# Earlier loads for one block, and a last output tile in two column groups: attention with sinks and a window, then a feed-forward layer

## The chip, the cores and the metric

The kernel runs on one NeuronCore of a Trainium2 chip, in one launch. The metric is the device time in microseconds (us); lower is better. A profiled execution also gives a span, from its first to its last instruction, which is about 2 us shorter than its time.

The engines have their own instruction streams and wait for each other through semaphores: TensorE (PE in the profile; its weight loads are PEld), VectorE (DVE), ScalarE (ACT), GpSimd (POOL) and SyncE (SP). SP computes nothing here; it issues most of the transfers (DMAs), in program order.

## The reference

Attention over 4 batches, 8 heads, 768 tokens and 64 values per head; each token sees the first 4 tokens (the sinks) and the last 128. Its result, 3072 tokens of 512 values, goes through a two-layer network with 2048 hidden values and the activation h * sigmoid(1.702 h).

```
scores = q @ k.T / 8                       # per batch and head, 768 x 768
keep   = (key < 4) | (0 <= query - key < 128)
a      = softmax(where(keep, scores, -1e9))
x      = (a @ v) as [3072 tokens, 512]
h      = x @ w_in                          # 512 -> 2048
out    = (h * sigmoid(1.702 * h)) @ w_out  # 2048 -> 512
```

All inputs and the output are float32; the kernel computes in float16 with float32 sums.

## The kernel before

The 3072 tokens are cut into 12 blocks of 256, numbered k = 0 to 11; three make a batch. A block goes through these steps, and three blocks are in work at a time (attention of one, first layer of the one before it, second layer of the one before that):

- **Loads.** `load(k)` brings q, k and v from HBM (float32). In blocks 0 to 3 q and k come in two halves of heads each, 256 KB (L389); from block 4 on each is one transfer of 512 KB (L396). v is one transfer of 512 KB in all blocks (L404). There are three slots of float32 buffers, so block 3 writes where block 0 was. SP issues nearly all of them.
- **Casts to float16** (L278), from block 2 on all on POOL, in the order q and k of a block, then v.
- **Turning q and k**, so that the head's values lie on partitions: in blocks 0 to 3 by TensorE transposes (L507) with copies out of PSUM by ACT or DVE (L278, tile `blkT`); from block 4 on by a DMA transpose (L529).
- **Scores** (L589) and scores against the sinks (L547) on TensorE, exp on ACT (L609, L555), the mask on DVE (L616), the product with v (L649), division by the sums on DVE (L667, L669), and turning the result (L688 and L695 in the first blocks, then a DMA transpose, L676).
- **First layer**, `mm1(k)`: matmuls of 256 columns (L716), tanh on ACT (L728), the rest of the activation on DVE (L730).
- **Second layer**, `mm2(k)`: for each of the two halves j of 128 tokens, 16 matmuls of 512 columns into one PSUM bank (L744), a scaling by 0.5 into the float32 tile `osb` (L762 on ACT, L764 on DVE), and two stores of 64 tokens each (L776). Only the very last tile is scaled by ACT and DVE together, each taking 256 of the 512 columns of the same bank; its second store is issued by ACT, all others by SP.

The weights come as eight transfers of 512 KB by POOL's software queue (L349): w0 to w3 are `w_in`, w4 to w7 are `w_out`. Until enough is loaded, TensorE runs matmuls of zeros (L822).

The order of the instructions on each engine is not written down by hand. Every step is entered as an operation with an engine, a length, what it depends on and a priority; the class `Plan` simulates the engines, the PSUM banks and the transfers, takes at each moment the operation with the best priority that could start, and puts the instructions down in that order. The engines then execute them strictly in it. So a change of a dependency or a length can change the order of everything after it.

The transfers have an order of their own (`loads`, sorted by priority: blocks 0 and 1, w0 to w5, block 2, w6 and w7, block 3, block 4 and so on) and gates: for each n from 10 to 31 a load (not a weight) waits until an earlier transfer has landed, the one found by walking back until at least 3.8 us of planned transfer time lie between. For block 3 this gives: q waits for the values of block 2; k and v wait for w6. For block 4, q, k and v wait for the first q piece, the first and the second k piece of block 3, and block 5's q waits for block 3's v. Independent of that, a DMA also waits for the one eight places before it in its kind of queue, whose semaphore it takes over.

Of the kernel before, what the change touches and what calls it, by code (L numbers as in the profile page):

```python
# [14 lines left out]
P = 128  # L15
# [179 lines left out]
def kernel(  # L195
# [69 lines left out]
    def f32(o, i=0):  # L265
        return bank[o.banks[i]]
# [70 lines left out]

    CAST_QK, CAST_V = OPT.get("QK", CAST_QK), OPT.get("V", CAST_V)
    o_w = {}
    loads, gates, o_first = [], [], []  # L340

    def weights(j, at):
        if j < 4:
# [31 lines left out]
    def load(k):  # L375
        b, r = divmod(k, R)
        sl = k % RS
        t0 = r * TB
        prio = load_at(f"a{k}")
        war = reuse("s32", sl) + ([o_m[k - 2, 0][-1]] if k > KT else [])  # L380
        dst, dv = qk32[sl], v32[sl]
        lq = {}
        for e, src in enumerate((q, k_ap)):
            eng, dma = ("ACT", nc.scalar) if k == 0 and e else ("SP", nc.sync)
            lq[e] = []
            if k < KT:
                for h in range(2):
                    def f(e=e, h=h, src=src, dma=dma):
                        return dma.dma_start(  # L389
                            dst[:, e].rearrange("p h i d -> p (h i d)")[:, 512 * h : 512 * h + 512],  # L390
                            src[b, h::2, t0 : t0 + TB].rearrange("p (g i) d -> g p (i d)", i=8),
                        )
                    lq[e].append(op(eng, 450, (700 if k < 2 else 850, 8), f, war, prio=prio + (h / 2 + e / 8 if k == 0 else e / 2 + h / 8), kind="load"))
            else:
                def f(e=e, src=src, dma=dma):
                    return dma.dma_start(dst[:, e], src[b, :, t0 : t0 + TB].rearrange("h (p i) d -> p h i d", i=2))  # L396
                lq[e].append(op(eng, 450, (1850, 64), f, war, prio=prio + e / 2, kind="load"))
            loads.extend(lq[e])
            for o in lq[e]:
                o.begin = 1.0 if k > 1 else 0.0  # L400
            if k == 1:
                o_first.extend(lq[e])
        def lv(dma, h):
            return lambda: dma.dma_start(dv[:, h], v[b, h, t0 : t0 + TB].rearrange("h (p i) d -> p h i d", i=2))  # L404

        o_lv = [op("SP", 450, (1850, 64), lv(nc.sync, slice(0, 8)), war,
                   prio=load_at("a1") + 1.5 + k / 8 if k < 2 else prio + 0.7, kind="load")]
        o_lv[0].begin = 1.0 if k > 1 else 0.0
        loads.append(o_lv[0])

        c16 = qk16[k % RQ]
        war = reuse("qk16", k % RQ)
        if k >= KT:
            C = slots(c16)
            for e in range(2):
                for j in range(2):
                    for i in range(2):
                        def f(eng, e=e, j=j, i=i):
                            copy(eng, C[64 * i : 64 * i + 64, e, :, j].rearrange("s p (h d) -> s p h d", h=2),
                                 dst[64 * j : 64 * j + 64, e, :, i].rearrange("s (p h) d -> s p h d", h=2))  # L420
                        o = plan.any(cast(512, CAST_QK[k]), f, lq[e] + war, prio=nominal(k - 1, -7), kind="cqk")
                        o_cqk[k, 2 * e + j, i] = o
        else:
            C = eights(c16)
            for h in range(2):
                for e in range(2):
                    def f(eng, e=e, h=h):
                        copy(eng, C[:, e, :, :, h].rearrange("s i a d -> s a i d"),
                             dst[:, e].rearrange("s h i d -> s (h i d)").rearrange("s (h a i d) -> s h a i d", h=2, a=4, i=2)[:, h])
                    o_cqk[k, e, h] = plan.any(cast(512, CAST_QK[k]), f, [lq[e][h]] + war,  # L430
                                              prio=nominal(k - 1, -7 + 2 * h) if k else NEVER + h, kind="cqk")
        for o in {id(x): x for (kk, _, _), x in o_cqk.items() if kk == k}.values():
            uses("s32", sl, o)
        w16 = v16[k % RV]
        war = reuse("v16", k % RV)


        w = H // len(o_lv)
        for n, o_l in enumerate(o_lv):
            got = []  # L440
            for j in range(2):
                for i in range(2):
                    def f(eng, j=j, i=i, h=slice(w * n, w * n + w)):
                        copy(eng, w16[64 * i : 64 * i + 64, j, h, 0:D], dv[64 * j : 64 * j + 64, h, i])
                    o = plan.any(cast(D * w, CAST_V[k]), f, [o_l] + war + [o_ones],
                                 prio=(nominal(k - 1, -4) if k else NEVER + 5 + n), kind="cv")
                    got.append(o)
                    uses("s32", sl, o)
            for p in range(w * n // 2, w * n // 2 + w // 2):
                o_cv[k, p] = got  # L450
        if r == 0:
            def f():
                for t in range(2):
                    for i in range(2):
                        nc.gpsimd.tensor_copy(
                            out=vs16[64 * t + 32 * i : 64 * t + 32 * i + 2, b, :, i],
                            in_=w16[64 * t : 64 * t + 2, 0, i::2],
                        )
            o_vs[b] = op("POOL", 1400, 1500, f, [*o_cv[k, 0], *o_cv[k, NP - 1], o_vs0], prio=nominal(k - 1, 0), kind="vs")
            uses("v16", k % RV, o_vs[b])  # L460
# [239 lines left out]
    n_o = [0]  # L700
# [33 lines left out]
    def mm2(k):  # L734
        b, r = divmod(k, R)
        g = gT[k % RG]
        for j in range(2):
            last_tile = k == NK - 1 and j == 1
            holder = []
            prev = None  # L740
            for s in range(NS):
                def f(s=s, j=j, holder=holder):
                    for Fi in (2 * s, 2 * s + 1):
                        nc.tensor.matmul(  # L744
                            f32(holder[0]), g[:, Fi, bass.ts(j, P)], w_out16[:, Fi],
                            start=(Fi == 0), stop=(Fi == NF - 1),
                        )
                deps = [o_g[k, s], o_w[4 + s // 2]] + ([prev] if prev else [])
                o = op("PE", 2 * pe_ns(512), pe_ns(512) + 512 / 2.4 + 166, f, deps,
                       prio=nominal(k + 1, 4 * j + s / 2) + 3, acq=None if s else ("o", 1), kind="mm2")  # L750
                uses("gT", k % RG, o)
                holder.append(o)
                prev = o
            oi = n_o[0] % RO
            n_o[0] += 1
            O = osb[oi]
            row = k * TB + j * P
            war = reuse("osb", oi)

            def f(e, O=O, holder=holder, c=slice(0, d_model)):  # L760
                if e == "ACT":
                    nc.scalar.mul(O[:, c], f32(holder[0])[:, c], 0.5)  # L762
                else:
                    nc.vector.tensor_scalar_mul(O[:, c], f32(holder[0])[:, c], 0.5)  # L764

            prio = nominal(k + 1, 4 * j + 4) + 4
            if not last_tile:
                o_c = [op("ACT", 477, 600, lambda f=f: f("ACT"), [holder[-1]] + war, prio=prio,
                          rel=[(holder[0], 0)], kind="oc")]
            else:  # L770
                o_c = [op(e, 270, 400, lambda f=f, e=e, c=c: f(e, c=c), [holder[-1]] + war, prio=prio, kind="oc")
                       for e, c in (("ACT", slice(0, 256)), ("DVE", slice(256, 512)))]
            for i in range(2):
                eng = "ACT" if last_tile and i else "SP"
                def f(O=O, i=i, row=row, dma=nc.scalar if eng == "ACT" else nc.sync):
                    dma.dma_start(  # L776
                        out[row : row + P, :].rearrange("(p i) f -> i p f", i=2)[i], O[64 * i : 64 * i + 64]
                    )
                o_d = op(eng, 590, (420, 4), f, o_c, prio=prio, kind="out")
                uses("osb", oi, o_d)  # L780
# [24 lines left out]
    for n, o in enumerate(loads):  # L805
        if o is o_w[0]:
            g = o_first[-1]
        elif o.kind == "load" and 10 <= n < 4 + 5 * KT + 8:
            m, ahead = n - 1, 0.0
            while ahead < 3800:  # L810
                ahead += next(iter(loads[m].engs.values()))[1][0]
                m -= 1
            g = loads[m]
        else:
            continue
        o.deps.append(g)
# [57 lines left out]
```

## Time and profile before

| What | Value |
|---|---|
| Median of 4 runs | 225.96 us (225.09 to 226.8) |
| Profiled execution | 226.24 us, span 224.2 us |
| TensorE busy | 217.6 us of the span (97%) |
| L716, L744 (the two layers' matmuls) | 100.3 us and 99.8 us busy |
| DMA moved | 36.36 MB, mean 162 GB/s |
| Last of TensorE, last landing of a store | about 219.45 us, 222.99 us |
| Block 2: v issued by SP, cast by POOL from | 29.37 us, 41.20 us |
| Block 3: q and k issued by SP from, keys cast by POOL until | 41.20 us, 48.97 us |

Busy time of TensorE counts a matmul until its result is written; since matmuls overlap, the sum of its rows is longer than the array's work, and a short hole can be hidden by the drain of the matmul before it. Rows of a timeline are: start, length, engine, line, operation, output and inputs, how many are merged, and in brackets the idle time of the engine before it with what ended it. Rows of waits are: total us, times, longest. Rows of stages give, for each engine, the busy us and in brackets the instructions, and at the end TensorE's clock, the transfers' load and GB/s.

### The profile page before, as it was taken

Reading aid. Unit: us, or ns where it says so; the run is one execution under the profiler, and the core shown is the slowest. Engines: PE = TensorE matmul, PEld = TensorE weight load, DVE = VectorE, ACT = ScalarE, POOL = GpSimd, SP = SyncE. Lnnn points to the kernel's source line nnn. Section 1 sums busy time; section 2 is a strip of 40 time slices with the busy share of each in tenths; the row PEclk is TensorE's granted clock in tenths of the full one; section 3 lists DMA queues with packets and bytes.
Section 4 is the critical chain, followed back from the end, with each engine's and each line's share of the span. In section 5 each row is a group of like instructions: output and inputs, shape, how many; then the busy total and the mean of one; then the engine's idle time right before and its main releaser. Section 6 shows DMA issues by size and latency. Waiting matters only on the chain.

```text
span 224.2 us, 5446 instructions
## 1 busy us (share of the span) xinstructions
PE 217.6 (97%) x2170; PEld 152.9 (68%) x2170; DVE 124.8 (56%) x272; ACT 132.4 (59%) x263; POOL 90.9 (41%) x158
## 2 busy tenths in 40 slices
PE   8999999999999999999999999999999999999991
PEld 8968877566757766766677667657667676666640
DVE  1685865577726755566555664665466565534400
ACT  3398456876648776565576477456567576444310
POOL 8299013538996495814806818408400000000000
PEclk9999999999999999999999999999999999999999
DMA  5999999499996999599399598498641411330232
GB/s 205 338 166 201 195 259 246 128 275 303 291 169 119 274 158 261 154 178 281 86 213 233 74 233 211 89 217 214 124 89 25 84 29 31 76 67 0 50 76 65
DMA packets 65704, 36.36 MB, mean 162 GB/s; under 512 B 27760, under 2 KB 60544, under 8 KB 65680
## 3 DMA queue, kind: packets, MB, share of 16 engines
q1 hardware_dynamic: 61040, 31.07, 58.2%
q0 software_dynamic: 4272, 4.29, 11.7%
q10 hardware_dynamic: 368, 0.66, 0.9%
q8 instruction: 17, 0.28, 0.5%
q14 instruction: 7, 0.06, 0.1%
HBM read 27.36 MB, written 6.29 MB: 150 GB/s over the span
## 4 chain that ended last, share of the span: by engine, by line
PE 93%; ACT 2%; DVE 2%; issue 0%; ACTq 0%
PE bank L716 38%; PE bank L744 36%; PE bank L649 6%; PE bank L589 5%; PE bank L822 4%; PE bank L547 2%; ACT at L609 1%; PE bank L507 1%; PE bank L688 1%; PE bank L582 1%; DVE at L616 1%; DVE xn L669 0%; ACT blkT L278 0%; DVE gT L730 0%; ACT th L728 0%
## 5 line engine op out<-in xcount | busy, mean ns | idle before, releaser
L716 PE MATMUL bank<-xT,w_in 128*128 128x256 f16 x768 | 100.3, 273 | 0.0
L744 PE MATMUL bank<-w_out,gT 128*128 128x512 f16 x384 | 99.8, 379 | 0.0
L730 DVE SCALAR_TENSOR_TENSOR gT<-th,bank 128x512 f16<-128x512 f16 x96 | 65.6, 684 | 46.6 <-ACT th L728 46.0
L716 PEld LDWEIGHTS <-w_in 128*128 128x128 f16 x768 | 72.6, 98 | 22.2 <-issue 2.5
L728 ACT ACTIVATE th<-bank 128x512 f16<-128x512 f32 x96 | 57.8, 602 | 45.1 <-PE bank L716 43.0
L278 POOL CAST qk<-qk 64x512 f16<-64x512 f32 (+1 forms) x73 | 44.5, 610 | 54.9 <-DMA qk<-in_q_dram 47.5
L609 ACT ACTIVATE at<-bank 128x512 f16<-128x512 f32 (+1 forms) x96 | 50.4, 572 | 14.6 <-PE bank L589 14.4
L744 PEld LDWEIGHTS <-gT 128*128 128x128 f16 x384 | 35.5, 98 | 23.1 <-issue 0.3
L616 DVE TENSOR_TENSOR at<-at,bank 128x1024 f16<-128x1024 f16 (+1 forms) x40 | 25.6, 639 | 22.3 <-ACT at L609 22.3
L278 POOL CAST v<-v 64x512 f16<-64x512 f32 x45 | 27.6, 614 | 7.7 <-DMA v<-in_v_dram 5.5
L649 PE MATMUL bank<-v,at 128*128 128x65 f16 x352 | 21.2, 193 | 0.2 <-DVE v L278 0.2
L762 ACT ACTIVATE osb<-bank 128x512 f32<-128x512 f32 (+1 forms) x24 | 14.2, 591 | 12.0 <-PE bank L744 12.0
L649 PEld LDWEIGHTS <-at 128*128 128x128 f16 x352 | 17.5, 98 | 3.7 <-DVE at L616 0.3
L555 ACT ACTIVATE ats<-bank 128x256 f16<-128x256 f32 x32 | 12.6, 394 | 7.6 <-PE bank L547 7.5
L669 DVE TENSOR_TENSOR xb<-bank,rcp 128x256 f16<-128x256 f32 x36 | 15.1, 421 | 0.6
L649 PE MATMUL bank<-vs,ats 128*128 128x65 f16 x128 | 14.8, 193 | 0.0
L667 DVE RECIPROCAL rcp<-bank 128x4 f32<-128x4 f32 x48 | 8.6, 179 | 9.6 <-PE bank L649 8.5
L589 PE MATMUL bank<-blkT 64*128 64x256 f16 x192 | 13.4, 244 | 0.0
L589 PEld LDWEIGHTS <-blkT 64*128 64x128 f16 x256 | 8.0, 94 | 7.7 <-issue 6.7
L649 PEld LDWEIGHTS <-ats 128*128 128x128 f16 x128 | 11.9, 97 | 1.9 <-issue 0.2
L822 PE MATMUL bank<-zero 128*128 128x128 f16 x99 | 8.4, 259 | 1.0 <-DVE zero L291 1.0
L547 PE MATMUL bank<-blkT,ks 128*128 128x256 f16 x32 | 8.7, 272 | 0.1
(41 smaller groups left out, 86.8 us busy)
## 6 DMA issues: line engine op xcount, KB each, us to landing
v<-in_v_dram SPq DMA_DIRECT2D x12, 512.0 KB, 6.8
out_dram<-osb SPq DMA_DIRECT2D x47, 128.0 KB, 2.7
qk<-in_q_dram SPq DMA_DIRECT2D x8, 512.0 KB, 5.2
qk<-in_k_dram SPq DMA_DIRECT2D x8, 512.0 KB, 5.8
qk<-in_q_dram SPq DMA_DIRECT2D x8, 256.0 KB, 4.7
w_in<-in_moe_w_in_dram POOLq DMA_DIRECT2D x4, 512.0 KB, 7.1
w_out<-in_moe_w_out_dram POOLq DMA_DIRECT2D x4, 512.0 KB, 14.8
qk<-in_k_dram SPq DMA_DIRECT2D x6, 256.0 KB, 5.0
```

What stands on the lines that cost most here:

```text
L278: {"POOL": nc.gpsimd.tensor_copy, "DVE": nc.vector.tensor_copy, "ACT": nc.scalar.copy}[e](out=out, in_=in_)
L589: nc.tensor.matmul(f32(o_s, 2 * n + i)[:, c : c + w], src[d, j], Q[d].rearrange("d j s -> d (j s)")[:, q0 : q0 + w], start=k >= KM, stop=T ...
L609: nc.scalar.activation(out=A[:, i, 0:W], in_=f32(o_s, 2 * n + i)[:, 0:W], func=AF.Exp, scale=scale)
L616: nc.vector.tensor_tensor(out=A[:, :, 0:W], in0=A[:, :, 0:W], in1=mask[:, c0 : c0 + W].unsqueeze(1).to_broadcast((P, 2, W)), op=ALU.mult,)
L649: nc.tensor.matmul(avp()[:, j, i], a_, v_, start=(n == 0), stop=(n == len(mms) - 1))
L669: o_n = op("DVE", 300, 425, lambda: nc.vector.tensor_tensor(out=X, in0=avp()[:, :, :, 0:D], in1=rc.to_broadcast((P, 2, 2, D)), op=ALU.mult ...
L716: nc.tensor.matmul(f32(holder[0])[:, bass.ts(e, TB)], w_in16[:, c, bass.ts(Fi, P)], X[:, c] if k < KX else X2[:, :, c], start=(c == 0), st ...
L728: o_t = op("ACT", 477, 600, lambda first=first: nc.scalar.activation(out=th[first.places[0]], in_=f32(first), func=AF.Tanh, scale=0.851), ...
L730: o_g[k, s] = op("DVE", 565, 690, lambda first=first, s=s: nc.vector.scalar_tensor_tensor(out=g[:, 2 * s : 2 * s + 2].rearrange("p a t -> ...
L744: nc.tensor.matmul(f32(holder[0]), g[:, Fi, bass.ts(j, P)], w_out16[:, Fi], start=(Fi == 0), stop=(Fi == NF - 1),)
L762: nc.scalar.mul(O[:, c], f32(holder[0])[:, c], 0.5)
L822: nc.tensor.matmul(warm_bank[:, 0:P], zero, zero, start=True, stop=True)
```

## The change

Two things are changed. First, the gates: only the loads with n from 10 to 22 (those of block 2 among them) keep the rule of 3.8 us. The q and k pieces of block 3 wait for block 2's last key piece alone; v of block 3, the loads of block 4 and q of block 5 have no gate left. Second, the last of the 24 output tiles: its 512 columns are computed as a group of 384 and then one of 128, each 16 matmuls, in two PSUM banks. ACT scales the first and SP stores it (two stores of 64 x 384); DVE scales the second, and SP and ACT store it (64 x 128 each). All other tiles are computed, scaled and stored as before. Weight loads on TensorE grow by 16, matmuls by 16, stores by 2.

```
-        elif o.kind == "load" and 10 <= n < 4 + 5 * KT + 8:
+        elif o.kind == "load" and 10 <= n < 15 + 8:
             m, ahead = n - 1, 0.0
             while ahead < 3800:
                 ahead += next(iter(loads[m].engs.values()))[1][0]
                 m -= 1
             g = loads[m]
+        elif o in o_third:
+            g = o_second[-1]
...
     def mm2(k):
-        for j in range(2):
-            last_tile = k == NK - 1 and j == 1
+        for j, c0, c1 in ((0, 0, 512), (1, 0, 512)) if k < NK - 1 else ((0, 0, 512), (1, 0, 384), (1, 384, 512)):
+            w = c1 - c0
...
                         nc.tensor.matmul(
-                            f32(holder[0]), g[:, Fi, bass.ts(j, P)], w_out16[:, Fi],
+                            f32(holder[0])[:, 0:w], g[:, Fi, bass.ts(j, P)], w_out16[:, Fi, c0:c1],
                             start=(Fi == 0), stop=(Fi == NF - 1),
                         )
...
-                    nc.scalar.mul(O[:, c], f32(holder[0])[:, c], 0.5)
+                    nc.scalar.mul(O[:, c0:c1], f32(holder[0])[:, 0:w], 0.5)
                 else:
-                    nc.vector.tensor_scalar_mul(O[:, c], f32(holder[0])[:, c], 0.5)
+                    nc.vector.tensor_scalar_mul(O[:, c0:c1], f32(holder[0])[:, 0:w], 0.5)
...
-            if not last_tile:
-                o_c = [op("ACT", 477, 600, lambda f=f: f("ACT"), [holder[-1]] + war, prio=prio,
-                          rel=[(holder[0], 0)], kind="oc")]
-            else:
-                o_c = [op(e, 270, 400, lambda f=f, e=e, c=c: f(e, c=c), [holder[-1]] + war, prio=prio, kind="oc")
-                       for e, c in (("ACT", slice(0, 256)), ("DVE", slice(256, 512)))]
+            e = "DVE" if c0 else "ACT"
+            o_c = [op(e, w / 1.2 + 50, w / 1.2 + 170, lambda f=f, e=e: f(e), [holder[-1]] + war, prio=prio,
+                      rel=[(holder[0], 0)], kind="oc")]
             for i in range(2):
-                eng = "ACT" if last_tile and i else "SP"
+                eng = "ACT" if c0 and i else "SP"
```

As the planner sees the loads of block 3 and 4 at other times, it puts the instructions from about 44 us of its plan in another order: on TensorE the transposes of block 3 (L507) stand some places earlier between the score, value and second-layer matmuls of block 2's attention; on ACT a copy into `blkT` stands ahead of the last exp steps of block 2; on DVE copies, masks and reciprocals change places; on SP the first output stores stand behind all of block 4's loads. POOL's order is unchanged.

More of the change, by code (lines that the diff above doesn't have):

```diff
@@ L339 @@
     o_w = {}
-    loads, gates, o_first = [], [], []
+    loads, gates, o_first, o_second, o_third = [], [], [], [], []
     def weights(j, at):
@@ L400, in load @@
                 o.begin = 1.0 if k > 1 else 0.0
-            if k == 1:
-                o_first.extend(lq[e])
+            if k in (1, 2, 3):
+                (o_first, o_second, o_third)[k - 1].extend(lq[e])
         def lv(dma, h):
@@ L736, in mm2 @@
         g = gT[k % RG]
-        for j in range(2):
-            last_tile = k == NK - 1 and j == 1
+        for j, c0, c1 in ((0, 0, 512), (1, 0, 512)) if k < NK - 1 else ((0, 0, 512), (1, 0, 384), (1, 384, 512)):
+            w = c1 - c0
+            last = w < d_model
             holder = []
@@ L741, in mm2, with f @@
             for s in range(NS):
-                def f(s=s, j=j, holder=holder):
+                def f(s=s, j=j, holder=holder, c0=c0, c1=c1, w=w):
                     for Fi in (2 * s, 2 * s + 1):
                         nc.tensor.matmul(
-                            f32(holder[0]), g[:, Fi, bass.ts(j, P)], w_out16[:, Fi],
+                            f32(holder[0])[:, 0:w], g[:, Fi, bass.ts(j, P)], w_out16[:, Fi, c0:c1],
                             start=(Fi == 0), stop=(Fi == NF - 1),
@@ L748, in mm2 @@
                 deps = [o_g[k, s], o_w[4 + s // 2]] + ([prev] if prev else [])
-                o = op("PE", 2 * pe_ns(512), pe_ns(512) + 512 / 2.4 + 166, f, deps,
-                       prio=nominal(k + 1, 4 * j + s / 2) + 3, acq=None if s else ("o", 1), kind="mm2")
+                o = op("PE", 2 * pe_ns(w), pe_ns(w) + w / 2.4 + 166, f, deps,
+                       prio=nominal(k + 1, 4 * j + s / 2) + 3 + c0 / 100 * L, acq=None if s else ("o", 1), kind="mm2")
                 uses("gT", k % RG, o)
@@ L753, in mm2, with f @@
                 prev = o
-            oi = n_o[0] % RO
-            n_o[0] += 1
+            if not c0:
+                oi = n_o[0] % RO
+                n_o[0] += 1
+                war = reuse("osb", oi)
             O = osb[oi]
             row = k * TB + j * P
-            war = reuse("osb", oi)
-            def f(e, O=O, holder=holder, c=slice(0, d_model)):
+            def f(e, O=O, holder=holder, c0=c0, c1=c1, w=w):
                 if e == "ACT":
-                    nc.scalar.mul(O[:, c], f32(holder[0])[:, c], 0.5)
+                    nc.scalar.mul(O[:, c0:c1], f32(holder[0])[:, 0:w], 0.5)
                 else:
-                    nc.vector.tensor_scalar_mul(O[:, c], f32(holder[0])[:, c], 0.5)
+                    nc.vector.tensor_scalar_mul(O[:, c0:c1], f32(holder[0])[:, 0:w], 0.5)
             prio = nominal(k + 1, 4 * j + 4) + 4
-            if not last_tile:
-                o_c = [op("ACT", 477, 600, lambda f=f: f("ACT"), [holder[-1]] + war, prio=prio,
-                          rel=[(holder[0], 0)], kind="oc")]
-            else:
-                o_c = [op(e, 270, 400, lambda f=f, e=e, c=c: f(e, c=c), [holder[-1]] + war, prio=prio, kind="oc")
-                       for e, c in (("ACT", slice(0, 256)), ("DVE", slice(256, 512)))]
+            e = "DVE" if c0 else "ACT"
+            o_c = [op(e, w / 1.2 + 50, w / 1.2 + 170, lambda f=f, e=e: f(e), [holder[-1]] + war, prio=prio,
+                      rel=[(holder[0], 0)], kind="oc")]
             for i in range(2):
-                eng = "ACT" if last_tile and i else "SP"
-                def f(O=O, i=i, row=row, dma=nc.scalar if eng == "ACT" else nc.sync):
+                eng = "ACT" if c0 and i else "SP"
+                def f(O=O, i=i, row=row, c0=c0, c1=c1, dma=nc.scalar if eng == "ACT" else nc.sync):
                     dma.dma_start(
-                        out[row : row + P, :].rearrange("(p i) f -> i p f", i=2)[i], O[64 * i : 64 * i + 64]
+                        out[row : row + P, c0:c1].rearrange("(p i) f -> i p f", i=2)[i], O[64 * i : 64 * i + 64, c0:c1]
                     )
```

## The prediction

> **What bounds the kernel now.** I read the page's engine table first, then TensorE's waits, then three stretches of the timeline: the loads between 28 and 50 us, TensorE around 49 us, and the end.
>
> ```profile
> span 224.2 us, 5446 instructions
> PE 217.6 (97%) x2170; PEld 152.9 (68%) x2170; DVE 124.8 (56%) x272; ACT 132.4 (59%) x263; POOL 90.9 (41%) x158
> ```
>
> TensorE is busy for all but 6.6 us, and 4.7 of those are the end: its last matmul ends at about 219.45 of 224.2. So no change of loads can give much; it can only close the few holes in TensorE's row. In the waits of matmuls and of weight loads between 40 and 50 us one place stands out, the transposes of block 3 (L507):
>
> ```profile
> PE bank L507 <- DVE xn L669: 0.4, 1, 0.4
> PEld L507 <- POOL qk L278: 0.9, 1, 0.9
> ```
>
> The timelines of TensorE and of POOL say what it is:
>
> ```profile
> 47.63 1.02 PE L744 MATMUL bank<-w_out,gT 128*128 128x512 f16 x4
> 49.03 0.62 PE L507 MATMUL bank<-perm,qk 128*128 128x128 f16 x8 [0.38 <-DVE xn L669]
> ```
> ```profile
> 36.52 0.61 POOL L278 CAST qk<-qk 128x512 f16<-128x512 f32 x1 [0.71 <-DMA qk<-in_k_dram]
> 41.20 2.61 POOL L278 CAST v<-v 64x512 f16<-64x512 f32 x4 [4.07 <-DMA v<-in_v_dram]
> 44.31 1.18 POOL L278 CAST qk<-qk 128x512 f16<-128x512 f32 x2 [0.49 <-PE bank L649]
> 46.84 0.61 POOL L278 CAST qk<-qk 128x512 f16<-128x512 f32 x1 [1.35 <-DMA qk<-in_k_dram]
> 48.36 0.61 POOL L278 CAST qk<-qk 128x512 f16<-128x512 f32 x1 [0.91 <-DMA qk<-in_k_dram]
> ```
>
> The last cast of block 3's keys ends at 48.97 and the transposes start at 49.03. Four 512-column matmuls from 47.63 fill the array for 4 x 0.216 = 0.86 us, to 48.49. The hole is 0.54 us (the timeline prints 0.38, since it counts a matmul's drain as busy). The keys are late because of SP's gates, in its own timeline:
>
> ```profile
> 29.37 0.59 SPq L404 DMA_DIRECT2D v<-in_v_dram  x1
> 41.20 1.18 SPq L389 DMA_DIRECT2D qk<-in_q_dram  x2
> 42.48 1.20 SPq L389 DMA_DIRECT2D qk<-in_k_dram  x2
> ```
>
> SP stands from 29.96 to 41.20 for block 2's values (11.8 us from issue to landing). By stages the transfers nearly stop there:
>
> ```profile
> 38.00:39.00 1.00, 1.00 (x15) 0.94 (x14) 1.00 (x2) 0.58 (x1) 0.00 (x0) 1.00 1.06 278
> 39.00:41.20 2.20, 2.20 (x19) 1.41 (x19) 1.03 (x3) 1.53 (x3) 0.00 (x0) 1.00 0.19 48
> 41.20:42.50 1.30, 1.25 (x17) 0.83 (x17) 0.59 (x1) 0.90 (x2) 1.22 (x2) 1.00 0.00 0
> ```
>
> The last number is GB/s: 278, 48, 0. At the end:
>
> ```profile
> 219.47 0.38 ACT L762 ACTIVATE osb<-bank 128x256 f32<-128x256 f32 x1 [2.85 <-PE bank L744]
> 219.89 0.42 DVE L764 TENSOR_SCALAR osb<-bank 128x256 f32<-128x256 f32 x1 [6.87 <-ACT osb L762]
> 220.35 0.56 ACTq L776 DMA_DIRECT2D out_dram<-osb  x1
> ```
>
> The two halves of the last tile are scaled one after the other, DVE waiting for ACT, and both stores (SP's at 220.34, ACT's at 220.35) go out after both.
>
> **What the Trainium skill says.** (1) "PSUM — Partial Sum Buffer", section "PSUM bank collisions raise a hardware error": two engines may not touch one bank together, reads included, so ACT and DVE are ordered against each other. The trace agrees: DVE starts 0.04 us after ACT ends. (2) "TensorE: Matmul & The Clock Gate", section "Wait — 56ns, not 53.3ns?": a warm matmul costs N/2.4 + 2.5 ns. It agrees: 36 matmuls of 512 in 7.78 us are 216 ns each, 8 of 128 columns in 0.45 us are 56. (3) "DMA: Bandwidth & Descriptors", section "Queues, rings and completion order": an engine takes one queue's descriptors in order, and turns between queues. It agrees: block 2's four q and k pieces were all issued by 29.3 and were cast at 32.3, 33.6, 35.2, 36.5, in turn, while the software queue's w_out ran beside them. (4) Same page, "Anatomy of one DMA — SWDGE (gpsimd) path": a DMA's fixed part is mostly the receipt of its last write (told of the software path; no run here splits it). In the trace 128 KB stores take 2.2 to 2.6 us to land, though two issued in a row land only 0.65 apart.
>
> **Part 1, the loads.** Removed: block 3's q and k no longer wait for block 2's values or for w_out's third quarter, and block 3's values, block 4's loads and block 5's q have no gate of this kind. Added: block 3's q and k wait for block 2's last keys, landed by 36.5 (their cast starts at 36.52). SP then issues four pieces at 0.6 us each, 36.5 to 39.0, instead of 41.2 to 43.7. They stand behind block 2's values in SP's queue, so they run when those are done, about 41. A 256 KB piece takes 0.65 to 1.4 us (spacing of the landings of block 3's q, and of block 2's casts): q lands by about 42.5, k by about 44 (before: 48.3). Behind SP's four are v, then block 4's q, k, v, then the first output stores, now after block 4's v. That v waits for block 2's values (its semaphore lane, landed 41.2), so the stores are issuable by 42 to 47; ACT writes the first at 44.05 to 44.7 and needs that slot again three tiles later, so I cost their shift at nothing.
>
> POOL keeps its order: v of block 2 from 41.20 to 43.81, then block 3's four casts at about 0.63 each, done at 46.3 instead of 48.97. POOL is then the limit, not the DMA.
>
> In the changed instruction order TensorE has L507 for q just after the key-sink matmul at 46.14, and for k after that, 46.28 + 0.45 (L507) + 0.11 (L688) + 0.86 (four L744) + 0.37 (L649) = 48.07. The casts are done 1.8 us before: the hole of 0.54 closes. What is late next is DVE's last mask of block 2, for the L649 that follows: it needs ACT's exp, which now stands behind a blkT copy (0.48) and ends at about 48.1; mask 0.59, so 48.75, while TensorE comes at 48.95. Slack 0.2, so between 0 and 0.2 of the 0.54 may come back. Past 50 us I find no hole but the turnaround of each score group, so nothing more is to be won. Part 1: -0.5 us, bounds -0.6 and (rival A) +3.
>
> **Part 2, the last tile.** TensorE: 16 x 162.5 + 16 x 56 = 3.50 us for 16 x 216 = 3.45, so +0.03 to +0.05; the 16 more weight loads are inside the 56 ns (L507's row has one each). On the old clock: the 384 columns are ready at 218.57, ACT scales them from 218.60 in 0.49 (between 0.38 for 256 and 0.60 for 512), SP issues at 219.13 and 219.64 (0.46 and 0.59 each with 0.05 between, as at 216.65). TensorE ends at 219.48, DVE needs no ACT now and takes about 0.30 (its rows of 4 and of 256 elements take 0.18 and 0.42, L667 and L669), ACT issues its 32 KB at 219.82, SP its own only at 220.28, after its two larger ones. So SP's last issue is hardly earlier than today (220.34); the gain is size. Before: the last landing was 220.35 + 2.64 = 222.99. After: the two 96 KB land at about 221.3 and 221.95 (0.65 apart), SP's 32 KB 0.2 later, 222.15; ACT's 219.82 + 2.2 = 222.0. Gain 0.84; if a small store takes the full 2.4 it lands at 222.7, gain 0.3; if nothing queues, 1.0. I take **-0.75**.
>
> **Sum.** -0.5 - 0.75 + 0.04 = -1.2 us. The profiled execution took 226.24 (span 224.2 and 2.0 around it), so 225.0; it lay 0.28 above the median of the four runs, 225.96, which gives **224.7**.
>
> **Rivals.** A measurement of this kernel can tell about 0.5%, 1.13 us, from no change.
> A, slower: block 3's q and k take engine time from block 2's values. Those have no slack: their last cast ends at 43.81 and the first L649 that reads them starts at 43.82, so each us of delay stalls TensorE by one. If the engines shared evenly, 1 MB at the 272 GB/s seen after 42.5 is 3.9 us: +3.9 - 0.54 - 0.7 = +2.6, 228.6. It decides the sign from a delay of 1.25 us, and slower by 0.5% from 2.4. Against it: the pieces of one queue were served in turn, and at 39 us little of the values was left. A small delay of 0.3 to 0.5 (fewer free engines for the stragglers) is likelier: 225.1. Chances 0.06 for 1.25 us or more, 0.2 for the small one.
> B, part 1 gives nothing: the L507 hole was as much DVE's as POOL's (the page names xn, ended at 49.0), and the wait moves to the mask: only the tail, 225.2. For it: the 0.2 us of slack. Chance 0.14.
> C, the tail gives little, since SP's last issue stays where it was: -0.5 - 0.3, 225.2. Chance 0.15.
> D, the likeliest, 0.45: both parts, 224.7, own range 224.1 to 225.2.
>
> **Range and chances.** The best bounds, -0.6 and -1.0, give 224.4, and the scatter of the runs shown, 225.09 to 226.8, asks for some more: 223.9. Upward I take in B, C, and A up to a delay of 1.6 us: 226.4. Faster by over 0.5% (under 224.83): most of D and a little of the others, 0.54; within 0.5%: 0.40; slower: 0.06.
>
> **What would show it.** Right: SP's q and k of block 3 issued at about 36.5; POOL's casts of block 3 without a gap after those of v; no idle time before L507 near 48 us; TensorE's end 0.5 us earlier; DVE's last copy no longer waiting for ACT; the last landing under 2.8 us after TensorE's end (3.5 before). Wrong: v of block 2 cast later than 41.5 (A), a new TensorE wait on DVE's mask (B), or SP's last store landing over 3.2 us after TensorE's end (C).

## The result and the profile after

| | Before | After |
|---|---|---|
| Median of the runs | 225.75 us (60 runs, 224.69 to 227.7) | 224.81 us (41 runs, 223.97 to 225.39) |
| Ratio after / before | | 0.9952, 95% interval 0.9941 to 0.9962 |
| Profiled execution | 226.24 us, span 224.2 | 225.26 us, span 223.3 |
| End of TensorE, last landing of a store | 219.44, 222.99 us | 219.46, 222.32 us |

The change saves 0.0048 x 225.75 = 1.08 us (0.86 to 1.33); the forecast was 1.2 us and 224.7. This is about the half per cent that was named as the bound of what can be told, and its interval is clear of no change.

The page of the changed kernel has the same picture as before, a TensorE that is nearly always busy:

```profile
span 223.3 us, 5479 instructions
PE 218.0 (98%) x2186; PEld 154.5 (69%) x2186; DVE 124.9 (56%) x272; ACT 132.9 (59%) x263; POOL 90.7 (41%) x158
```

The timeline of SP after, the first place to look at for the loads (start, length, issuing engine, line, what is loaded, how many):

```profile
36.59 1.19 SPq L389 DMA_DIRECT2D qk<-in_q_dram  x2
37.83 1.25 SPq L389 DMA_DIRECT2D qk<-in_k_dram  x2
```

Block 3's q and k are issued at 36.59, at the landing of block 2's last keys, and no longer at 41.20. The view by stages after shows that the transfers go on where before they nearly stopped (its last number is GB/s: 278, 48, 0 before):

```profile
38.00:39.00 1.00, 1.00 (x13) 0.74 (x11) 0.59 (x1) 0.51 (x2) 0.00 (x0) 1.00 1.17 247
39.00:41.20 2.20, 2.20 (x21) 1.78 (x19) 1.39 (x3) 1.58 (x4) 0.00 (x0) 1.00 1.10 357
41.20:42.50 1.30, 1.24 (x17) 0.66 (x16) 0.77 (x2) 0.77 (x2) 0.78 (x2) 1.00 1.06 379
```

POOL's timeline after (the casts) and then TensorE's:

```profile
36.59 0.61 POOL L278 CAST qk<-qk 128x512 f16<-128x512 f32 x1 [0.66 <-DMA qk<-in_k_dram]
41.66 2.61 POOL L278 CAST v<-v 64x512 f16<-64x512 f32 x4 [4.46 <-DMA v<-in_v_dram]
44.33 2.28 POOL L278 CAST qk<-qk 128x512 f16<-128x512 f32 x4
46.56 2.61 POOL L278 CAST v<-v 64x512 f16<-64x512 f32 x4
```
```profile
48.53 0.22 PE L649 MATMUL bank<-v,at 128*128 128x65 f16 x2
48.60 0.61 PE L507 MATMUL bank<-perm,qk 128*128 128x128 f16 x8
49.04 0.59 PE L745 MATMUL bank<-w_out,gT 128*128 128x512 f16 x2
```

From 44.33 on POOL has no bracket any more: it waits for no transfer, and casts block 3's q, k and v in one go. The keys are cast by 46.61, 2.4 us earlier than before (48.97), and the transposes at 48.60 follow the matmuls ahead of them without a bracket. The hole of 0.54 us is gone.

And the end, in the timeline of all engines after:

```profile
218.60 0.49 ACT L764 ACTIVATE osb<-bank 128x384 f32<-128x384 f32 x1 [2.00 <-PE bank L745]
219.12 1.75 SPq L775 DMA_DIRECT2D out_dram<-osb  x3
219.50 0.29 DVE L766 TENSOR_SCALAR osb<-bank 128x128 f32<-128x128 f32 x1 [6.50 <-DMA out_dram<-osb]
219.82 0.55 ACTq L775 DMA_DIRECT2D out_dram<-osb  x1
```

DVE starts 0.04 us after TensorE's end and no longer behind ACT (its bracket names a store; but the last store before it landed at 219.52, when DVE had already started, and it is TensorE's end that DVE follows). SP has three issues in a row, from 219.12 to 220.87; the third, of 32 KB, begins at about 220.32 and lands last, at 222.32. That is 2.86 us after TensorE's end, and it was 3.55 before: 0.69 us gained.

One thing does not fit at first sight: with the hole gone, TensorE should end 0.5 us earlier, and it ends where it did. The two timelines differ from the start. The first transposes (L507), before and then after:

```profile
8.32 0.61 PE L507 MATMUL bank<-perm,qk 128*128 128x128 f16 x8
```
```profile
8.85 0.61 PE L507 MATMUL bank<-perm,qk 128*128 128x128 f16 x8
```

The matmuls of zeros that warm TensorE up start 107 ns apart and then, from one to the next, 56 ns apart: from 5.64 us on before and from 6.72 us on after. So they ran at half speed about 1 us longer in the profiled execution after, and everything that follows on TensorE is 0.53 us later, up to the first products with block 2's values (L649: 44.32 against 43.79). The missing hole then makes up for just this. From the start of L507 to the end of TensorE it is 219.46 - 8.85 = 210.61 us after and 219.44 - 8.32 = 211.12 before. The Trainium skill, "TensorE: Matmul & The Clock Gate", section "What's actually happening", says that the clock is released in a window that runs free of the kernel's start, so that the moment varies by 0.5 us either way. That it varies, the traces here show too, but by more: over the fourteen of them the matmuls come 56 ns apart from a moment between 3.7 and 6.8 us on, and the first L507 starts anywhere between 7.48 and 8.87 us. What two single traces say is compared from L507 on below, with one more caution: a TensorE that is early can be ahead of its first loads, as in the loads-alone kernel (L507 at 7.48), whose waits near 14 and 16 us are 1.01 us together against 0.84 after.

### The profile page after: what moved, and what is told of

It reads as the page before. It is cut to its first block, busy times and chain, and to the rows that moved or that the text cites. A ratio compares the mean times of both kernels' runs of the same rounds, so it can differ in the third digit from the quotient of the medians.

```text
span 223.3 us, 5479 instructions
## 1 busy us (share of the span) xinstructions
PE 218.0 (98%) x2186; PEld 154.5 (69%) x2186; DVE 124.9 (56%) x272; ACT 132.9 (59%) x263; POOL 90.7 (41%) x158
## 4 chain that ended last, share of the span: by engine, by line
PE 93%; ACT 2%; DMA 1%; DVE 1%; issue 0%; SPq 0%; ACTq 0%
PE bank L716 38%; PE bank L745 35%; PE bank L649 6%; PE bank L589 5%; PE bank L823 4%; PE bank L547 2%; ACT at L609 1%; PE bank L507 1%; DMA out_dram<-osb 1%; PE bank L688 1%; PE bank L582 1%; ACT blkT L278 0%; DVE gT L730 0%; ACT osb L764 0%; ACT th L728 0%
## 5 line engine op out<-in xcount | busy, mean ns | idle before, releaser
L745 PE MATMUL bank<-w_out,gT 128*128 128x512 f16 (+2 forms) x400 | 100.2, 370 | 0.0
L278 POOL CAST qk<-qk 64x512 f16<-64x512 f32 (+1 forms) x73 | 44.3, 609 | 53.9 <-DMA qk<-in_q_dram 43.5
L745 PEld LDWEIGHTS <-gT 128*128 128x128 f16 x400 | 36.4, 98 | 21.9 <-issue 0.3
L278 POOL CAST v<-v 64x512 f16<-64x512 f32 x45 | 27.6, 614 | 6.8 <-DMA v<-in_v_dram 4.5
L649 PE MATMUL bank<-v,at 128*128 128x65 f16 x352 | 21.1, 193 | 0.2 <-DVE v L278 0.2
L649 PEld LDWEIGHTS <-at 128*128 128x128 f16 x352 | 17.6, 98 | 4.0 <-issue 0.3
L649 PE MATMUL bank<-vs,ats 128*128 128x65 f16 x128 | 14.8, 193 | 0.0
L649 PEld LDWEIGHTS <-ats 128*128 128x128 f16 x128 | 11.9, 97 | 2.2 <-ACT th L728 0.2
L823 PE MATMUL bank<-zero 128*128 128x128 f16 x99 | 8.9, 269 | 1.0 <-DVE zero L291 1.0
L823 PEld LDWEIGHTS <-zero 128*128 128x128 f16 x99 | 8.4, 124 | 1.0 <-DVE zero L291 1.0
```

What stands on the lines that cost most here:

```text
L278: {"POOL": nc.gpsimd.tensor_copy, "DVE": nc.vector.tensor_copy, "ACT": nc.scalar.copy}[e](out=out, in_=in_)
L649: nc.tensor.matmul(avp()[:, j, i], a_, v_, start=(n == 0), stop=(n == len(mms) - 1))
L745: nc.tensor.matmul(f32(holder[0])[:, 0:w], g[:, Fi, bass.ts(j, P)], w_out16[:, Fi, c0:c1], start=(Fi == 0), stop=(Fi == NF - 1),)
L823: nc.tensor.matmul(warm_bank[:, 0:P], zero, zero, start=True, stop=True)
```

## The experiments

Each ratio is against the kernel before, run on the same chip.

**The loads alone.** The theory behind the forecast is that the two parts add, 0.5 us of loads and 0.75 of the end. The kernel is the one before with the new gates only:

```
-        elif o.kind == "load" and 10 <= n < 4 + 5 * KT + 8:
+        elif o.kind == "load" and 10 <= n < 15 + 8:
...
+        elif o in o_third:
+            g = o_second[-1]
```

> The new gates alone, the last tile as before. Theory (the two parts act apart, each on its own piece of the chain): block 3's keys are cast by about 46.8 us, the 0.54 us hole before the k transposes (L507) closes, nothing takes its place: 0.54 us less, ratio about 0.9976; the last store still lands 3.5 us after TensorE's end. Rival (the wait moves to DVE's mask or copies): TensorE's end stays, ratio 1.000. Rival (block 2's values land later because of the loads behind them): over 1.000.

Measured: 225.53 us, ratio 0.9992 (0.9981 to 1.0003), a gain of 0.18 us with an interval from -0.07 to 0.43 (the plain medians of these runs and of those before, 225.87, lie 0.34 us apart). The last landing stays 3.56 us after TensorE's end. The trace has no hole between 40 and 56 us, and in its timeline of TensorE the transposes again follow without a bracket:

```profile
47.43 0.61 PE L507 MATMUL bank<-perm,qk 128*128 128x128 f16 x8
47.88 0.59 PE L744 MATMUL bank<-w_out,gT 128*128 128x512 f16 x2
```

So the gates did in the trace what was forecast, but the runs do not show 0.5 us for it, and do not tell the gain from zero.

**The end alone.** The changed kernel with the old gates:

```
-        elif o.kind == "load" and 10 <= n < 15 + 8:
+        elif o.kind == "load" and 10 <= n < 4 + 5 * KT + 8:
...
-        elif o in o_third:
-            g = o_second[-1]
```

> The two column groups alone, gates as before. Theory: the hole of 0.54 us before L507 is still there, and the last store lands 2.85 us after TensorE's end instead of 3.54: 0.68 us less, ratio about 0.9970. Rival (the whole gain of the change is from the loads): 1.000, the rest of the change's 1.08 us then has to be in the loads alone, 0.9952. If the parts add, the two ratios' gains sum to that of both, 0.0048.

Measured: 225.06 us, ratio 0.9965 (0.9952 to 0.9978), a gain of 0.79 us; the last landing is 2.86 us after TensorE's end, as in the changed kernel. The two gains add to 0.97 us, within the interval of the whole change; what is left for the loads of the whole change is 1.08 - 0.79 = 0.29 us. The surprise is in the trace. The old gates stand in it, yet there is no hole before the transposes. It stands 4 us later, in the products with block 3's values, as TensorE's timeline and then POOL's show:

```profile
52.96 0.25 PE L649 MATMUL bank<-v,at 128*128 128x65 f16 x3 [0.28 <-POOL v L278]
```
```profile
50.30 2.61 POOL L278 CAST v<-v 64x512 f16<-64x512 f32 x4 [2.31 <-DMA v<-in_v_dram]
```

POOL waited 2.31 us for the values, which the old gates bring late too, and TensorE stood 0.45 us (start to start; the bracket is shorter since the drain of the matmul before counts as busy).

**Is the hole the same in every execution?** This suggested that 0.54 us is one draw and no constant. Three more profiles of the kernel before, unchanged:

> The kernel before, once more, for its trace. Theory (the hole that late loads of block 3 make in TensorE's row differs from run to run, since it depends on how the transfers before them fell): the hole between 44 and 56 us is not always 0.54 us; 0 to 0.6, before L507 or before the first L649 that reads block 3's values. Rival (it is 0.54 us every time, and the new gates lose most of it again elsewhere): 0.45 to 0.6 us in each look.

> As the first look at the kernel before: theory a hole of 0 to 0.6 us, rival 0.45 to 0.6 us.

> As the first look at the kernel before: theory a hole of 0 to 0.6 us, rival 0.45 to 0.6 us.

Measured: 225.31, 225.8 and 225.17 us. In the first of them, TensorE's timeline has no hole at all before L507, since (POOL's timeline, second fence) the keys are cast by 47.34:

```profile
47.44 1.02 PE L744 MATMUL bank<-w_out,gT 128*128 128x512 f16 x4
48.30 0.61 PE L507 MATMUL bank<-perm,qk 128*128 128x128 f16 x8
```
```profile
46.08 1.26 POOL L278 CAST qk<-qk 128x512 f16<-128x512 f32 x2 [1.38 <-DMA qk<-in_k_dram]
```

The second has none between 40 and 56 us either, but its waits of TensorE name another, near 33 us and thus ahead of everything that the gates move, for a quarter of `w_out`:

```profile
PE bank L744 <- DMA w_out<-in_moe_w_out_dram: 0.3, 1, 0.3
```

The third has 0.15 us at 52.44, before L649, for block 3's values. All executions together, holes of TensorE between 40 and 56 us (from the start of one matmul to the start of the next, less the time of the first in the array; a step of 0.22 us at 41 to 43 us, which every trace has, is left out). The kernels that have not been named yet come below, and the one with an extra load is not in the table:

| Gates | Execution | Hole | First L507 to TensorE's end |
|---|---|---|---|
| old | before | 0.54 us, keys of block 3 | 211.12 us |
| old | before, further profile 1 | none | 210.57 |
| old | before, further profile 2 | none (0.49 at 33 us for `w_out`) | 211.33 |
| old | before, further profile 3 | 0.15, values of block 3 | 210.72 |
| old | end alone | 0.45, values of block 3 | 211.05 |
| new | after | none | 210.61 |
| new | after, second run | none | 210.61 |
| new | loads alone | none | 210.77 |
| new | last stores from ACT | none (1.53 at 30 to 35 us for `w_out`) | 212.12 |
| new | last stores from ACT, second run | none | 210.61 |
| new | two groups of 256 | none (0.67 at 33 us for `w_out`) | 211.27 |
| new, none on block 3's q and k | no gate | none | 210.61 |
| new, none on block 3's q and k | both together | none | 210.62 |

With the old gates the hole is 0.54, 0, 0, 0.15 and 0.45 us, on the mean 0.23; with the new ones it is zero in all eight. (A wait for `w_out` makes TensorE late, and so can hide a late load behind it; this bears on one of the five and on two of the eight.) The last column agrees: without a hole and without a wait for `w_out` it is 210.57 us with the old last tile (further profile 1) and 210.61 or 210.62 with the new one, and the holes and waits come on top. The loads alone have 0.17 us more of early waits, as said above. The new gates leave room besides: in the trace after, block 3's keys are cast 2.0 us and its values 3.6 us ahead of TensorE (46.61 and 48.60, 49.17 and 52.78).

So the new gates take away a wait that comes in some executions, and the 0.18 us timed for the loads alone is near the mean, not near the 0.54, though five executions fix a mean only roughly. The gates also changed the order in which TensorE takes its instructions; no run separates the earlier loads from the new order. For the keys the order alone could not take the wait away, since it asks for them earlier (at 48.60 - 0.53 = 48.07 us on the clock of before, where TensorE was free for them at 48.49).

**The issuing engine of the last stores.** Rival C said that SP's row of issues holds up the end. Here ACT issues the second 96 KB store, so SP has two in a row and not three:

```
-                eng = "ACT" if c0 and i else "SP"
+                eng = "ACT" if last and i else "SP"
```

> The changed kernel, but ACT also issues the second store of the 384 columns, so SP issues one of each group. Theory (SP's row of three issues sets the end: its last one starts at 220.32 though the data are ready at 219.79): both last issues start at about 219.82, last landing about 0.2 to 0.4 us earlier, ratio about 0.994. Rival (the completion of a store, whoever issues it, or the transfers ahead of it in the queues set the end): the last landing stays at about 2.85 us after TensorE's end, ratio as the changed kernel, 0.9952.

Measured: 224.44 us, ratio 0.9940 (0.9920 to 0.9961), and 224.60 us, 0.9943 (0.9925 to 0.9962), in a second comparison beside the changed kernel, which then gave 224.67 us and 0.9949 (0.9928 to 0.9969):

> The changed kernel with ACT issuing the second store of the 384 columns as well, beside the changed kernel on one chip. Theory: 0.39 us less than the changed kernel, as the last landings say (2.47 against 2.86 us after TensorE's end): its ratio less 0.0017. Rival (the first ratio of 0.994 was luck): the same ratio as the changed kernel.

> The changed kernel once more, beside the next two, so that they can be compared with it on one chip. Theory: ratio 0.995 to 0.996, no hole in TensorE's row between 40 and 56 us, last landing 2.86 us after TensorE's end. Rival (its gain over the tail alone, 0.9965, was luck): 0.9965 or more.

The end of it, from the timeline:

```profile
220.29 1.16 SPq L775 DMA_DIRECT2D out_dram<-osb  x2
220.29 1.39 ACTq L775 DMA_DIRECT2D out_dram<-osb  x2
220.67 0.29 DVE L766 TENSOR_SCALAR osb<-bank 128x128 f32<-128x128 f32 x1 [6.49 <-DMA out_dram<-osb]
```

Both 96 KB stores go out at 220.29 and SP's row ends 0.5 us after DVE (in the changed kernel 1.1 us after). The last landing is 2.47 us after TensorE's end in both traces, 0.39 less than in the changed kernel. The ratios lie 0.0006 to 0.0012 lower, 0.14 to 0.27 us, with intervals that overlap: the traces show the gain, the timing does not tell it from zero. (This profiled execution took 226.13 us and ended TensorE at 220.63, since it stood 1.5 us for `w_out` at 30 to 35 us, like the further profile 2 above.)

**The widths of the groups.** Two groups of 256 in place of 384 and 128:

```
-((0, 0, 512), (1, 0, 384), (1, 384, 512))
+((0, 0, 512), (1, 0, 256), (1, 256, 512))
```

> The changed kernel with two groups of 256 columns instead of 384 and 128. DVE's copy is 0.42 us instead of 0.29, the last stores are 64 KB instead of 32, but SP's first two issues are over by 219.3. Theory (SP's row of issues sets the end with 384 and 128): last issues at 219.95, 0.37 us earlier than 220.32, minus about 0.15 to 0.2 for the larger data: last landing 0 to 0.25 us earlier, ratio 0.9940 to 0.9952. Rival (size of the last store and length of the last copy set the end): 0.3 us later than the changed kernel, ratio 0.9965.

Measured: 224.64 us, ratio 0.9944 (0.9923 to 0.9965), last landing 2.69 us after TensorE's end. From its timeline of the end:

```profile
219.14 0.42 DVE L766 TENSOR_SCALAR osb<-bank 128x256 f32<-128x256 f32 x1 [6.49 <-DMA out_dram<-osb]
219.59 0.56 ACTq L775 DMA_DIRECT2D out_dram<-osb  x1
```

DVE's copy takes 0.42 and not 0.29 us, but the first group is done earlier, so SP's first two issues are over before DVE is. So the gain does not need a small last group; what this kernel shares with the changed one are two groups computed one after the other in two banks, scaled by two engines that do not wait for each other. (This execution too waited for `w_out`, 0.67 us.)

**How much room do block 2's values have?** Rival A said none. An added 512 KB load goes ahead of them in SP's queue; it brings the same values into a tile that nothing reads, and the order of the computation is the same:

```
+                if k == 2:
+                    dma.dma_start(extra, v[b, h, t0 : t0 + TB].rearrange("h (p i) d -> p h i d", i=2))
```

> The changed kernel with one more transfer of 512 KB (block 2's values, into a tile that nobody reads) issued by SP just ahead of block 2's values; the order on the compute engines is as in the changed kernel. Theory (block 2's values have no slack, so TensorE stands for as long as they are late): they land 1.5 to 2.5 us later, a hole of 1.3 to 2.5 us before L649 near 44 us, and the time is longer than the changed kernel's by about as much, ratio 1.001 to 1.007. Rival (there is slack of a us or more, or the engines make it up later): ratio at most 0.998.

Measured: 225.85 us, ratio 1.0002 (0.9981 to 1.0022), so about 1.1 us more than the changed kernel, and just below the range expected. TensorE's timeline, then POOL's (the added lines move the numbers: L654 is L649 of the changed kernel, and L279 its L278):

```profile
44.57 0.19 PE L654 MATMUL bank<-v,at 128*128 128x65 f16 x1 [0.78 <-POOL v L279]
```
```profile
41.91 2.61 POOL L279 CAST v<-v 64x512 f16<-64x512 f32 x4 [5.93 <-DMA v<-in_v_dram]
```

The values are cast from 6.55 us after block 2's last keys, against 4.6 to 5.1 in the six traces with the new gates and without this load. What counts is when TensorE needs them. It begins the group of products at 43.4, gets through five of its eight, and stands 0.94 us from 43.60 to 44.57 (start to start), until the last cast is over at 44.52. So a cast that ends 1.1 us after the group's start costs 0.94 us: some 0.2 us found room. Rival A's mechanism is real, and its price of one us per us was nearly right; the hole expected before this run, 1.3 to 2.5 us, was too large. What rival A needs is a delay, and the next experiment asks whether loads queued behind make one.

**Block 3's q and k without any gate.** The changed kernel without

```
-        elif o in o_third:
-            g = o_second[-1]
```

> The changed kernel without any gate on block 3's q and k: SP issues them right behind block 2's values, some 6 us earlier. Theory (SP's queue serves its transfers in turn, so loads that stand behind block 2's values cannot delay them): block 2's values land about 5 us after its last keys as in the changed kernel, same ratio within 0.001. Rival (transfers issued early take engine time from those ahead): block 2's values land 1 us or more later, a hole before L649 near 44 us, ratio 0.999 or more.

Measured: 224.41 us, ratio 0.9941 (0.9926 to 0.9957). SP's timeline, then POOL's:

```profile
28.91 0.59 SPq L404 DMA_DIRECT2D v<-in_v_dram  x1
29.60 2.85 SPq L389 DMA_DIRECT2D qk<-in_q_dram  x2
32.50 1.41 SPq L389 DMA_DIRECT2D qk<-in_k_dram  x2
```
```profile
35.37 0.61 POOL L278 CAST qk<-qk 128x512 f16<-128x512 f32 x1 [0.78 <-DMA qk<-in_k_dram]
40.84 2.61 POOL L278 CAST v<-v 64x512 f16<-64x512 f32 x4 [4.86 <-DMA v<-in_v_dram]
43.52 2.28 POOL L278 CAST qk<-qk 128x512 f16<-128x512 f32 x4
```

One MB now stands behind block 2's values from 29.6 us on, and they are cast 5.47 us after the last keys, 0.4 us later than after the change (41.66 - 36.59 = 5.07) and 0.8 later than before (41.20 - 36.52 = 4.68). But the other traces scatter as much: 4.3 to 4.8 us in the five with the old gates, 4.6 to 5.1 in the six with the new ones, and 4.62 in the next kernel, which has no gate either. From issue to landing the values take 11.9 us here, 11.5 in the next kernel, and 11.0 to 11.8 with the old gates. No hole came of it. So the gate on block 3's q and k is not needed for the time. A delay of block 2's values by the loads behind them, rival A, is not shown; the 3.9 us of an even sharing is excluded.

**Both together**, the last stores from ACT and no gate:

> The changed kernel with ACT issuing the second store of both groups, and no gate on block 3's q and k: the two edits that were not worse, together. Theory: only the stores' edit is worth something, 0.39 us (0.0017), so 0.993 to 0.994, last landing 2.47 us after TensorE's end. Rival (the removed gate gives more, as its single ratio of 0.9941 beside 0.9949 could mean): 0.9925 or less.

Measured: 224.53 us, ratio 0.9939 (0.9918 to 0.9959), last landing 2.47 us after TensorE's end, and no hole. This is not told apart from either edit alone, nor from the change.

## Why the prediction was right, and where it was off

- **Part 1, the path of the loads**: right step by step. SP's q and k were issued at 36.59 (36.5 forecast), POOL cast block 3 without a gap, done by 46.61 (46.3), and the transposes of the keys started at 48.60: the forecast 48.07 plus the 0.53 us by which this execution was late from the start. TensorE's end, forecast 0.5 us earlier, stayed in the profiled execution, and is 0.51 us earlier counted from the first L507.
- **Part 1, the size**: the term that was mis-sized. "The hole of 0.54 closes" was true of the one execution shown; as a gain of the median it should have been the mean hole, 0.23 us over five executions, and 0.18 us was timed (-0.07 to 0.43, so 0.5 is out). That execution lay 0.28 us above the median of the four runs shown, and 0.49 above that of all 60. The forecast took the 0.28 from the end result as a shift, but left the hole whole. It also looked for lateness of the keys alone; the values of block 3, late under the same gates, were where two of the five stood.
- **Part 2**: the term of 0.75 measured 0.69 in the landings and 0.79 in the runs. Its instants held: ACT's issue at 219.82 to the hundredth, DVE's copy 0.29 for 0.30, SP's last issue about 220.32 for 220.28. The last landing came 0.17 us later than the 222.15 worked out, so the cut from 0.84 to 0.75 was in the right direction. The forecast's "the gain is size" is only half of it: ACT's last store took 2.33 us to land instead of 2.64, but it also went out at 219.82 instead of 220.35, since DVE no longer holds it up. Sent at 220.35 it would have landed at 222.68 (an estimate from these numbers), 0.31 us earlier than before instead of 0.67.
- **The sum**: 0.18 + 0.79 = 0.97 us by the separate timings, 1.08 for the whole, 1.2 forecast. What is missing to the forecast is part 1, and part 2 gave a little more than its 0.71 us (0.75 less 0.04 for TensorE). That 224.7 came within 0.1 us of 224.81 is partly luck: the sum started from the median of four runs, 225.96, which was 0.21 us above that of all 60. From 225.75 it gives 224.5.
- **Rival A** did not come. Block 2's values were cast from 41.66, just past the mark of 41.5 that was to tell it, but in an execution that was 0.53 us late on TensorE too, and no wait followed. The mark should have been a time relative to TensorE's work. That lateness helped here; the loads-alone kernel, whose TensorE was 0.84 us ahead of the one before, has no wait there either. "No slack" was close: the room is some 0.2 us.
- **Rival B**: no wait on DVE's mask was seen near 49 us; part 1 did give little, but not by this mechanism. The wait was often not there to be removed.
- **Rival C**: SP's row of three issues did set the last landing, but at 2.86 us after TensorE's end, below its mark of 3.2. In the traces it costs 0.39 us, as moving one issue to ACT shows; the timing does not resolve that.

What stays open: whether ACT's issue or the missing gate is faster than the change at all, since the intervals overlap; how large the gain of the loads alone is, since its interval holds zero. Why a quarter of `w_out` lands up to 3 us later in some executions (27.1 to 30.3 us for the first) was not followed up; it costs TensorE 0.5 to 1.5 us where it happens, with old gates and new.

## What to carry to other kernels

A hole read from one profile is one draw: before you book it as a gain of the median, look at a few more profiles of the same kernel, and compare them from a fixed instruction on, not from the start of the span. Where transfers just make it in time, moving them earlier removes a wait that comes and goes, and is worth its mean. At the end of a kernel count the issues in a row on each engine after the last matmul, and give each engine that copies a bank of its own.

## What the runs showed of the hardware

- The moment from which TensorE's matmuls of zeros run at full speed (56 ns apart and no longer 107) differs by about 3 us between executions of these kernels (3.7 to 6.8 us). The first L507 moves by about half of that (7.48 to 8.87 us), and so does the end where nothing behind it is late; single profiles can't show half a us of gain without taking this out.
- Loads queued behind others in SP's queue were not seen to delay them: with 1 MB and more issued behind them block 2's values, a load of 512 KB, were cast from 4.6 to 5.5 us after the keys ahead of them, and from 4.3 to 4.8 us with nothing behind them until they had landed. A 512 KB load ahead of it made this 6.55 us.
- A small store is hardly quicker to land: at the end of these kernels, from issue to landing, the 32 KB stores took 1.9 to 2.0 us (SP) and 2.1 to 2.3 (ACT), the 96 KB ones 2.1 to 2.2 and 2.4, the 128 KB ones 2.2 to 2.4 and 2.6.
